# Adding up a tile's partial outputs in the second and third step of the following tile instead of the first and second

## The chip, the cores and the metric

The kernel runs on one core of one Trainium2 chip. The metric is the device time of one execution in microseconds (us), the median over several runs. The engines are called by the profile's names: PE (TensorE matmul) with PEld (its weight loads), DVE (VectorE), ACT (ScalarE), POOL (GpSimd) and SP (SyncE, which here only issues DMAs). A "q" behind an engine's name, as in SPq, is its sequencer.

## What is computed

Two branches over the same input of 2048 rows of 512 numbers, mixed by a gate per row. Branch A is an attention that goes through the rows in 64 segments of 32 and carries an 8-row memory from one segment to the next, so its segments can only be computed one after the other. Branch B is a layer norm with a two-layer MLP.

```python
for s in range(n_seg):                                   # 64 segments of 32 rows
    h = concat([mem, x[s*32:(s+1)*32]])                  # 8 memory rows + 32 rows
    q, k, v = h @ Wq, h @ Wk, h @ Wv                     # 32 heads of 128
    p = softmax(where(mask, q @ k.T * scale, -1e9))
    o = (p @ v) @ Wo                                     # 40 rows of 512
    mem = o[:8]                                          # carried on
    a[s] = o[8:]
b = gelu(layernorm(x) @ w1 + b1) @ w2 + b2
g = sigmoid((x * gate_w).sum(-1))
return g * a + (1 - g) * b
```

## The kernel before

**Tiles and steps.** 128 rows make a tile `T` (16 tiles), four segments make up a tile, and each segment `s = 4T + si` is one pass of the loop at line 694, called a step here; "the first step of a tile" is `si = 0`. Branch B runs ahead of the loop for all rows and leaves `(1 - g) * b` in DRAM (`c_dr`). The loop then takes some 10 us a step, and its order is written out by hand: each engine does its instructions in the order in which the code issues them, and waits on semaphores where an operand is not ready. The order within DVE's own instructions is therefore fixed by the code, and so is the order of the DMAs on SP.

**A step on PE.** Queries and keys of the step (line 124, into the PSUM banks `U`, from the transposed input `hT` of the step), scores (294, 298), values (143), sums of the exponentials (305, 308, 645), the product with the values (318, 323), then `wo_pass` (lines 674 to 680, matmuls at 155 into the bank `W`) and three little products (`new_mem`, line 688), from which DVE copies the new memory rows into the next step's `hT` (line 690). The first query matmul of the next step needs these copies. Between these parts PE runs work of the neighbouring tile that nothing in the step waits for (the generator `fill`: `left_qk`, `left_v`, `wo_left`).

**A delayed normalisation.** The softmax sums of the 32 ordinary rows are not divided out within the step. DVE takes the reciprocal (656), SP writes it to DRAM (659, `r_dr`) and reads it back spread over all partitions (660, `Rb`, 512 KB), and in the following step POOL multiplies (`x_norm`, line 672) the raw product `XR` by it into `UT` and `UL`. `wo_pass` of the following step reads that `UT`. After this POOL adds to `racc` (664) and copies parts of the next queries and inputs (278 `prep_q`, 274 `prep_h`).

**Outputs by parts.** What `wo_pass` leaves (`w`, 128 x 512) holds a step's output rows as four partial sums, one per group of heads. SP writes it to DRAM (`put_w`, line 243, in the step after the next) and reads it back so that the four parts of a row lie side by side in the tile `G` (`get_w`, 252; in each step of tile T + 1, the buffers of `G` are two). Eight rows of each segment come by another way: `wo_left` computes them a tile later, `put_left` (246) writes them to `l_dr` in the last step of tile T + 1, and `get_left` (254 to 257) reads them into `G` by four DMAs in the first step of tile T + 2. In that step SP also issues a DMA transpose of an input tile (`load_xT`, 98) while tiles are left to load.

**The addition.** `add_parts` (259 to 270) is a generator with four pieces: three additions of 128 x 512 (261, 263, 265) and a last one (268) that multiplies by the gate, adds `c`, and has SP store the tile (269). Lines 785 and 786 take two pieces in each step until none is left, right after `x_raw`; on DVE they stand behind `mask_put(0)` (287, called at 663) and ahead of the copies of line 690. The tiles 0 to 13 are finished in this way, 14 times; the last two tiles otherwise.

```python
        if si == 0 and T >= 2:
            get_left(T - 2)
            adds = add_parts(T - 2)
...
        x_raw(s)
        for _ in range(2):
            next(adds, None)
```

Of the kernel before, what the change touches and what calls it, by code (L numbers as in the profile page):

```python
# [27 lines left out]
def kernel(ctx, tc, A_x, A_mem0, A_Wq, A_Wk, A_Wv, A_Wo, A_seg_len, B_x, B_w1, B_b1, B_w2, B_b2, gate_w, out):  # L28
# [67 lines left out]
    def load_xT(T):  # L96
        xT = ew.tile([P, KC, P], BF16, tag="xT", bufs=3, name="xT")
        nc.sync.dma_start_transpose(out=xT[:], in_=x2[T * P:(T + 1) * P, :])
        xTs[T] = xT
# [21 lines left out]
    def qk_unit(bk, G, t, hf, kc):  # L121
        h0, h1 = HF[hf]
        for j in range(4):
            nc.tensor.matmul(bk[32 * j:32 * j + 32, :], lhsT=G[:, kc, :], rhs=W5[t][:, kc, h0:h1, j, :],  # L124
                             start=(kc == 0), stop=(kc == KC - 1), tile_position=(0, 32 * j))
# [37 lines left out]
    def flush(q, n=1):  # L163
        for _ in range(min(n, len(q))):
            q.pop(0)()
# [17 lines left out]
    def vp_load(T, si):  # L183
        nc.sync.dma_start(VP[T % 2][:, si].rearrange("p v e -> p (v e)"), VLs[T][si:P:SPT].rearrange("p a v e -> p a (v e)"))
# [20 lines left out]
    def c_load(T):  # L205
        c = cw.tile([P, Dm], BF16, tag="c", name="c")
        nc.sync.dma_start(c[:], c_dr[T * P:(T + 1) * P, :])
        cs[T] = c
# [32 lines left out]
    def put_w(s, w):  # L241
        T, si = divmod(s, SPT)
        nc.sync.dma_start(w_dr[T % 2][si], w[:])

    def put_left(T):
        nc.sync.dma_start(l_dr[T % 2][:], wls.pop(T)[:])

    def get_w(s):
        T, si = divmod(s, SPT)
        if si == 0:  # L250
            Gs[T] = cw.tile([P, 4, Dm], BF16, tag="G", name="G")
        nc.sync.dma_start(Gs[T][seg * si:seg * si + RIDE], w_dr[T % 2][si].rearrange("(c r) e -> r c e", c=4)[M:32])

    def get_left(T):
        for si in range(SPT):
            nc.sync.dma_start(Gs[T][seg * si + RIDE:seg * si + seg],
                              l_dr[T % 2][:].rearrange("(c i m) e -> i m c e", c=4, i=SPT)[si])

    def add_parts(T):
        a, G = cw.tile([P, Dm], FP32, tag="acc", bufs=1, name="acc"), Gs.pop(T)  # L260
        nc.vector.tensor_tensor(out=a[:], in0=G[:, 0], in1=G[:, 1], op=ALU.add)
        yield
        nc.vector.tensor_tensor(out=a[:], in0=a[:], in1=G[:, 2], op=ALU.add)
        yield
        nc.vector.tensor_tensor(out=a[:], in0=a[:], in1=G[:, 3], op=ALU.add)
        yield
        o = cw.tile([P, Dm], BF16, tag="o", name="o")
        nc.vector.scalar_tensor_tensor(out=o[:], in0=a[:], scalar=g_all[:, T:T + 1], in1=cs.pop(T)[:], op0=ALU.mult, op1=ALU.add)
        nc.sync.dma_start(out2[T * P:(T + 1) * P, :], o[:])
        yield  # L270

    def prep_h(s):
        T, si = divmod(s, SPT)
        nc.gpsimd.tensor_copy(out=hT[s % 3][:, :, 0:RIDE], in_=xTs[T][:, :, seg * si:seg * si + RIDE])
# [10 lines left out]
    def mask_put(i2):  # L285
        c = 4 * EW + (NG + 2 * M if i2 == 0 else 0)
        nc.vector.tensor_copy(out=(SbF, W)[i2][:, 0:c], in_=MkF[:, 0:c])
# [337 lines left out]
    def side(T, si):  # L625
        gens = []
        if si == 2:
            if T >= 1:
                gens.append(wo_left(T - 1, X1))
        elif T + 1 < NT:  # L630
            gens = [[left_qk(T + 1, 0, 0, X1), left_qk(T + 1, 1, 0, X2)], [left_qk(T + 1, 0, 1, X1), left_qk(T + 1, 1, 1, X2)], [],
                    [left_v(T + 1, 0, X1), left_v(T + 1, 1, X2)]][si]
        return chain(*gens)
# [33 lines left out]
    def x_norm(s):  # L667
        T, si = divmod(s, SPT)
        XR, Rb = XRs.pop(s), Rbs.pop(s)[:].rearrange("p (c q) (h j) -> p h j c q", c=4, h=2)
        for out, o, a, b in ((UT[(s + 1) % 2], M, LEFT, 32), (UL[T % 2], LEFT * si, 0, LEFT)):  # L670
            for h in range(2):
                nc.gpsimd.tensor_tensor(out=out[:, :, 4 * h:4 * h + 4, o:o + b - a], in0=XR[:, :, 4 * h:4 * h + 4, a:b], in1=Rb[:, h, :, :, a:b], op=ALU.mult)  # L672
# [21 lines left out]
    for s in range(nseg):  # L694
        T, si = divmod(s, SPT)
        last = s == nseg - 1
        hc, hn = hT[s % 3], hT[(s + 1) % 3]
        fill = side(T, si)
        if s + 1 < nseg:
            prep_h(s + 1)  # L700
        if s >= 1:
            x_norm(s - 1)
        if si == 0 and T >= 2:
            c_load(T - 2)
        if si < 3:
            vp_load(T, si + 1)
        if last:
            c_load(T - 1)
            c_load(T)
        if si == 0 and T + 2 < NT:  # L710
            load_xT(T + 2)
        if s >= 2 and s - 2 < SPT * (NT - 2):
            put_w(s - 2, ws.pop(s - 2))
        if 4 <= s < SPT * (NT - 2) + 4:
            get_w(s - 4)
        if si == 3 and 1 <= T < NT - 1:
            put_left(T - 1)
        if si == 0 and T >= 2:
            get_left(T - 2)
            adds = add_parts(T - 2)  # L720
        for n, (t, hf) in enumerate(((0, 0), (1, 0), (0, 1), (1, 1))):
            bk = U[n]
            for kc in range(KC):
                qk_unit(bk, hc, t, hf, kc)
            if n == 0:
                flush(act_q, 9)
                flush(dve_q, 9)
            qk_tr(qk_cast(bk[:]), (QT, KT)[t], hf, LEFT * (1 - t))
            if n == 0:
                mask_put(1)  # L730
        V = cw.tile([P, NG, Dh], BF16, tag="V", name="V")
        E = cw.tile([P, NG, EW], BF16, tag="E", name="E")
        R = cw.tile([P, NG * 40], FP32, tag="R", name="R")
        Rs[s] = R
        xsum = SbF[:, 0:32 * NG].rearrange("p (i q) -> p i q", q=32)

        def exps(i2, x):
            c = slice(0, 40) if x else slice(40, EW)
            nc.scalar.activation(out=E[:, 4 * i2:4 * i2 + 4, c], in_=Sb[i2][:, :, c], func=ACTF.Exp, scale=scale)  # L739

        def msum(i2):
            sums(U[i2][:, 320:352].rearrange("p (i q) -> p i q", q=8), E[:, 4 * i2:4 * i2 + 4, :], 40, 48, 8, True)

        def mnorm(i2):
            r, e = RP[i2], E[:, 4 * i2:4 * i2 + 4, 40:56].rearrange("p i (a q) -> p i a q", q=8)
            nc.vector.reciprocal(out=r, in_=U[i2][:, 320:352])
            nc.vector.tensor_tensor(out=e, in0=e, in1=r.rearrange("p (i q) -> p i q", q=8).unsqueeze(2).to_broadcast([P, 4, 2, 8]), op=ALU.mult)

        scores(s, 0)
        nc.scalar.activation(out=E[:, 0:4, :], in_=Sb[0], func=ACTF.Exp, scale=scale)  # L750
        for kc in range(KC):
            v_unit(X1, hc, 0, kc)

        def v_cast(vb, h):
            i0 = 4 * vb + 2 * h
            nc.scalar.copy(out=V[:, i0:i0 + 2, :].rearrange("p i e -> p (i e)"), in_=(X1, X2)[vb][:, 256 * h:256 * h + 256])  # L756

        v_cast(0, 0)
        v_unit(X2, hc, 1, 0)
        if not last:  # L760
            xsums(E, 0)
            msum(0)
            mnorm(0)
        scores(s, 1)
        exps(1, 0)
        v_cast(0, 1)
        exps(1, 1)
        for kc in range(1, KC - 1):
            v_unit(X2, hc, 1, kc)
        if not last:  # L770
            msum(1)
            mnorm(1)
        v_unit(X2, hc, 1, KC - 1)
        for h in range(2):
            v_cast(1, h)
        if last:
            break
        run(2)
        xsums(E, 1)
        recip_x(s)  # L780
        av(s, V, E)
        for j in (0, 2, 1, 3):
            nc.scalar.copy(out=UT[s % 2][:, j, :, 0:M], in_=U[j][:, 0:NG * 40].rearrange("p (i q) -> p i q", q=40)[:, :, 32:40])  # L783
# [3 lines that stand above are left out]
        run(2)  # L787
        prep_q(s + 1)
        w = wo_pass(UT[s % 2], (0, P, 2 * P, Dm))
        if s >= 1:  # L790
            ws[s - 1] = w
        run(2)
        new_mem(w, hn, 0)
        run(1)
        new_mem(w, hn, 1)
        run(1)
        new_mem(w, hn, 2)
        for _ in fill:
            pass
        if si == 3 and T + 2 < NT:  # L800
            left_x(T + 2)
        flush(dve_q, 9)
        nc.vector.tensor_tensor(out=rmin[:, 0:RW], in0=rmin[:, 0:RW], in1=R[:, 0:RW], op=ALU.min)
        flush(act_q, 9)
# [174 lines left out]
```

## Time and profile before

| | |
|---|---|
| median of 3 runs | 780.61 us (780.25 to 785.62) |
| the profiled execution | 785.22 us |
| its span, first to last instruction | 782.9 us |
| mean granted TensorE clock | 0.991 |
| busy PE / PEld / DVE / ACT / POOL | 754.3 / 410.5 / 425.3 / 538.6 / 291.5 us |

The profiled execution's time is 2.3 us above its span. The four pieces of the addition come 14 times each; in the view that groups instructions by line (busy time and mean duration, then the idle time of the engine just before, and what ended it) they are:

```profile
L268 DVE SCALAR_TENSOR_TENSOR o<-acc,g_all,c 128x512 bf16<-128x512 f32 x14 | 11.2, 798 | 0.5
...
L265 DVE TENSOR_TENSOR acc<-acc,G 128x512 f32<-128x512 f32 x14 | 10.0, 712 | 0.0
L263 DVE TENSOR_TENSOR acc<-acc,G 128x512 f32<-128x512 f32 x14 | 9.8, 698 | 0.5
L261 DVE TENSOR_TENSOR acc<-G 128x512 f32<-128x512 bf16 x14 | 9.7, 692 | 29.9 <-DMA r_dr<-R 23.5 <-DMA G<-l_dr 6.4
```

In a row of a timeline the first two numbers are the start and the duration in us, both of a merged group where the count behind the x is over one; a bracket tells for how long the engine sat idle before it and what ended that.

### The profile page before, as it was taken

The page shows a single profiled execution, that of the slowest core. Times are in us where ns is not written, and L with a number is a line of the kernel's source. Part 1 is how long each engine was busy: PE and PEld are TensorE (multiplying, and loading weights), DVE is VectorE, ACT ScalarE, POOL GpSimd, SP SyncE. Part 2 cuts the span into 40 slices and gives each one's busy share as a digit, 9 for nine tenths or more (in the row PEclk, how much of TensorE's full clock was granted, in tenths as well). Part 3 has the DMA queues.
Part 4 walks back from the last instruction along what each step waited for, and adds up shares of the span by engine and source line. Part 5 has one row for each costly group of instructions (what it writes and reads, how often), then busy time and mean ns, then how long its engine had stood idle before and what let it go on. Part 6 is the DMA issues. An engine that isn't in the chain of part 4 may idle for free.

```text
span 782.9 us, 43891 instructions
## 1 busy us (share of the span) xinstructions
PE 754.3 (96%) x19074; PEld 410.5 (52%) x19074; DVE 425.3 (54%) x1470; ACT 538.6 (69%) x1631; POOL 291.5 (37%) x522
## 2 busy tenths in 40 slices
PE   7999999999999999999999899999999999999997
PEld 5666555554555555555545455555545555555443
DVE  5776354555555464646455455646464655555454
ACT  4666676776777777777767567777767776777663
POOL 4111034443434444434344333444333443434441
PEclk9999999999999999999999999999999999999999
DMA  6779421324332323334243332233332323332212
GB/s 194 274 242 399 129 80 48 98 91 112 99 111 86 82 95 112 98 96 114 73 94 93 110 94 82 90 112 94 97 112 75 97 89 111 98 105 86 81 41 59
DMA packets 71687, 87.10 MB, mean 111 GB/s; under 512 B 23545, under 2 KB 61410, under 8 KB 69954
## 3 DMA queue, kind: packets, MB, share of 16 engines
q1 hardware_dynamic: 69762, 81.36, 33.6%
q8 instruction: 151, 2.47, 1.4%
q0 software_dynamic: 784, 1.97, 0.8%
q10 hardware_dynamic: 944, 0.92, 0.4%
q14 instruction: 46, 0.38, 0.2%
HBM read 64.30 MB, written 13.63 MB: 100 GB/s over the span
## 4 chain that ended last, share of the span: by engine, by line
PE 88%; DMA 3%; ACT 2%; DVE 2%; SPq 2%; issue 2%; POOL 1%; DVEq 0%; ACTq 0%; POOLq 0%
PE U L124 28%; PE X L143 17%; PE W L155 14%; PE X L124 6%; PE U L503 5%; PE U L318 4%; PE X L155 3%; PE W L497 2%; PE SbF L497 2%; PE U L305 1%; PE W L294 1%; DMA r_dr<-R 1%; PE U L688 1%; ACT w L679 1%; PE SbF L294 1%
## 5 line engine op out<-in xcount | busy, mean ns | idle before, releaser
L672 POOL TENSOR_TENSOR UT<-XR,Rb 128x384 bf16<-128x384 bf16 x126 | 139.9, 1132 | 321.4 <-DMA Rb<-r_dr 279.3
L129 ACT CAST Tb<-U 128x512 bf16<-128x512 f32 x258 | 151.2, 586 | 94.1 <-PE U L124 93.7
L124 PEld LDWEIGHTS <-hT 128*32 128x32 bf16 x4096 | 104.5, 97 | 115.2 <-DVE hT L690 20.5
L124 PE MATMUL U<-Wq_sb,hT 128*32 128x512 bf16 x2048 | 137.2, 383 | 11.8 <-DVE hT L690 11.8
L143 PE MATMUL X<-Wv_sb,hT 128*32 128x512 bf16 x2048 | 144.2, 378 | 0.6 <-issue 0.6
L124 PE MATMUL U<-Wk_sb,hT 128*32 128x512 bf16 x2048 | 133.6, 381 | 0.0
L155 PE MATMUL W<-Wo_sb,UT 128*32 128x512 bf16 x2080 | 126.9, 384 | 1.7 <-POOL racc L664 1.2
L133 DVE STREAM_TRANSPOSE QT<-Tb 128x256 f32<-128x256 f32 x128 | 57.1, 446 | 85.2 <-ACT Tb L129 85.2
L756 ACT CAST V<-X 128x256 bf16<-128x256 f32 x256 | 88.7, 372 | 16.4 <-PE X L143 4.6
L155 PEld LDWEIGHTS <-UT 128*32 128x32 bf16 x2080 | 56.7, 97 | 60.8 <-issue 17.6
L690 DVE CAST hT<-U 128x8 bf16<-128x8 f32 x126 | 19.7, 164 | 116.1 <-PE U L688 111.2
L679 ACT CAST w<-W 128x128 bf16<-128x128 f32 (+1 forms) x192 | 46.0, 311 | 48.9 <-PE W L155 48.9
L651 ACT CAST XR<-U 128x256 bf16<-128x256 f32 x252 | 78.4, 434 | 0.0
L133 DVE STREAM_TRANSPOSE KT<-Tb 128x256 f32<-128x256 f32 x128 | 57.0, 445 | 28.9 <-ACT Tb L129 24.4
L672 POOL TENSOR_TENSOR UL<-XR,Rb 128x128 bf16<-128x128 bf16 x126 | 60.7, 506 | 0.0
L143 PEld LDWEIGHTS <-hT 128*32 128x32 bf16 x2048 | 46.1, 94 | 23.1 <-issue 2.2
L503 PE MATMUL U<-w_sb,hTm 128*128 128x512 bf16 (+1 forms) x176 | 52.5, 382 | 0.0
L664 POOL TENSOR_TENSOR racc<-racc,R 128x72 f32<-128x72 f32 x63 | 22.6, 359 | 76.6 <-PE U L323 62.7
L783 ACT CAST UT<-U 128x64 bf16<-128x64 f32 x252 | 35.3, 226 | 22.9 <-PE U L323 22.9
L497 PEld LDWEIGHTS <-w_sb 128*128 128x128 bf16 (+1 forms) x352 | 34.4, 102 | 19.9 <-issue 1.3
L739 ACT ACTIVATE E<-W 128x64 bf16<-128x64 f32 (+1 forms) x128 | 35.0, 273 | 12.2 <-PE W L298 12.1
L688 PEld LDWEIGHTS <-w 128*32 128x32 bf16 x1008 | 22.8, 93 | 37.1 <-ACT w L679 29.1
(160 smaller groups left out, 1231.8 us busy)
## 6 DMA issues: line engine op xcount, KB each, us to landing
Rb<-r_dr SPq DMA_DIRECT2D x63, 512.0 KB
w_dr<-w SPq DMA_DIRECT2D x56, 128.0 KB
G<-w_dr SPq DMA_DIRECT2D x56, 96.0 KB
Wv_sb<-in_A_Wv_dram SPq DMA_DIRECT2D x4, 1024.0 KB
Wq_sb<-in_A_Wq_dram SPq DMA_DIRECT2D x4, 1024.0 KB
Wk_sb<-in_A_Wk_dram SPq DMA_DIRECT2D x4, 1024.0 KB
Wo_sb<-in_A_Wo_dram SPq DMA_DIRECT2D x4, 1024.0 KB
VP<-VL SPq DMA_DIRECT2D x64, 64.0 KB
```

The costliest lines, as they stand in the source:

```text
L124: nc.tensor.matmul(bk[32 * j:32 * j + 32, :], lhsT=G[:, kc, :], rhs=W5[t][:, kc, h0:h1, j, :], start=(kc == 0), stop=(kc == KC - 1), tile_ ...
L129: nc.scalar.copy(out=Tb[:], in_=bk.rearrange("p (a b e) -> p a e b", a=8, b=2))
L133: nc.vector.transpose(out=dst[:, 8 * hf:8 * hf + 8, c0:c0 + 32, :].rearrange("p a r b -> p a (r b)").bitcast(FP32), in_=Tb[:].rearrange("p ...
L143: nc.tensor.matmul(bk[32 * j:32 * j + 32, :], lhsT=G[:, kc, :], rhs=Wv5[:, kc, 4 * vb:4 * vb + 4, j, :], start=(kc == 0), stop=(kc == KC - ...
L155: nc.tensor.matmul(bk[32 * c:32 * c + 32, :], lhsT=U_[:, j, i, :], rhs=Wo_sb[:, 4 * i + j, :], start=(n == 0), stop=(n == NW - 1), tile_po ...
L497: nc.tensor.matmul(hp[:rows, 0:TB * P], lhsT=w1_sb[:, kc, fc * P:fc * P + rows], rhs=yTs[blk][:, kc, :], start=(kc == 0), stop=(kc == KC - 1))
L503: nc.tensor.matmul(bp(blk, tt)[:], lhsT=hTm[blk % 2][:rows, fc, tt * P:(tt + 1) * P], rhs=w2_sb[:rows, fc, :], start=(fc == 0), stop=(fc = ...
L651: nc.scalar.copy(out=XR[:, j], in_=U[j][:, 0:NG * 40].rearrange("p (i q) -> p i q", q=40)[:, :, 0:32])
L672: nc.gpsimd.tensor_tensor(out=out[:, :, 4 * h:4 * h + 4, o:o + b - a], in0=XR[:, :, 4 * h:4 * h + 4, a:b], in1=Rb[:, h, :, :, a:b], op=ALU ...
L679: nc.scalar.copy(out=w[:, a:b], in_=W[:, a:b])
L756: nc.scalar.copy(out=V[:, i0:i0 + 2, :].rearrange("p i e -> p (i e)"), in_=(X1, X2)[vb][:, 256 * h:256 * h + 256])
L783: nc.scalar.copy(out=UT[s % 2][:, j, :, 0:M], in_=U[j][:, 0:NG * 40].rearrange("p (i q) -> p i q", q=40)[:, :, 32:40])
```

## The change

The generator is made in the second step of a tile instead of the first. The loop at lines 785 and 786 still takes two pieces in a step, so lines 261 and 263 run in the second step instead of the first, and lines 265, 268 and the store of 269 in the third instead of the second. `get_left` stays where it is.

```diff
         if si == 0 and T >= 2:
             get_left(T - 2)
+        if si == 1 and T >= 2:
             adds = add_parts(T - 2)
```

The order on each engine shows that nothing else moves. On DVE the two pairs stand at the same place of their step as before, one step later. On SP the store of line 269 now comes behind five DMAs that it used to precede: the loads and stores of lines 184, 243 and 252, and the pair 659 and 660 of the third step. PE, ACT and POOL have the order they had. The number of instructions on each engine is unchanged.

## The prediction

> **What bounds the kernel.** I began with the page: the engines' busy shares, then the chain of waits followed back from the end.
>
> ```profile
> span 782.9 us, 43891 instructions
> ...
> PE 754.3 (96%) x19074; PEld 410.5 (52%) x19074; DVE 425.3 (54%) x1470; ACT 538.6 (69%) x1631; POOL 291.5 (37%) x522
> ...
> PE 88%; DMA 3%; ACT 2%; DVE 2%; SPq 2%; issue 2%; POOL 1%; DVEq 0%; ACTq 0%; POOLq 0%
> ```
>
> PE sets the time. DVE is busy 54% of it, and 40 us of additions on it cost nothing as such: they count only where PE stands still for them. So the next view is that of waits (who waited for what, total us, times, longest).
>
> ```profile
> DVE acc L261 <- DMA r_dr<-R: 23.5, 10, 3.5
> ...
> PE U L124 <- DVE hT L690: 11.8, 12, 2.1
> ...
> DVE acc L261 <- DMA G<-l_dr: 6.4, 3, 2.7
> ```
>
> Twelve times PE idles in front of the first query matmuls, for DVE's copies of the new memory: 11.8 us in all. Thirteen times DVE idles in front of the first addition, 29.9 us in all. That line reads nothing but `G`, so whichever DMA the view names, what it waits for is the landing of `get_left`. Whether the two belong together is seen in the timeline of tile 2, first on DVE and SP, then on PE; the rows from 196 us on are the second step, those from 207 us on the third.
>
> ```profile
> 185.55 0.42 DVE L287 CAST SbF<-MkF 128x248 f32<-128x248 bf16 x1
> 188.47 0.69 DVE L261 TENSOR_TENSOR acc<-G 128x512 f32<-128x512 bf16 x1 [2.50 <-DMA G<-l_dr]
> 189.20 0.69 DVE L263 TENSOR_TENSOR acc<-acc,G 128x512 f32<-128x512 f32 x1
> 189.81 0.23 DVE L690 CAST hT<-U 128x8 bf16<-128x8 f32 x2
> ...
> 197.31 0.68 DVE L265 TENSOR_TENSOR acc<-acc,G 128x512 f32<-128x512 f32 x1
> 198.03 0.80 DVE L268 SCALAR_TENSOR_TENSOR o<-acc,g_all,c 128x512 bf16<-128x512 f32 x1
> 199.95 0.43 DVE L690 CAST hT<-U 128x8 bf16<-128x8 f32 x2 [1.13 <-PE U L688]
> ...
> 207.19 0.42 DVE L287 CAST SbF<-MkF 128x248 f32<-128x248 bf16 x1
> 210.46 0.44 DVE L690 CAST hT<-U 128x8 bf16<-128x8 f32 x2 [2.85 <-PE U L688]
> ```
>
> ```profile
> 184.21 1.36 SPq L256 DMA_DIRECT2D G<-l_dr  x4
> ...
> 198.27 0.32 SPq L660 DMA_DIRECT2D Rb<-r_dr  x1
> 198.85 0.34 SPq L269 DMA_DIRECT2D out_dram<-o  x1
> ```
>
> ```profile
> 188.78 0.20 PE L688 MATMUL SbF<-SelM,w 128*32 128x8 bf16 x8
> 190.02 1.05 PE L124 MATMUL U<-Wq_sb,hT 128*32 128x512 bf16 x16 [1.03 <-DVE hT L690]
> ...
> 200.13 0.20 PE L688 MATMUL SbF<-SelM,w 128*32 128x8 bf16 x8
> 200.18 1.11 PE L124 MATMUL U<-Wq_sb,hT 128*32 128x512 bf16 x16
> ```
>
> In the first step SP has the four reads of `get_left` out by 185.57; DVE, free since 185.97, stands until 188.47, does both additions until 189.89, and only then gets to line 690, whose last operand PE had finished at 188.98. PE idles 1.03 us. In the second step the other two pieces start the moment DVE is free, end at 198.83, and DVE then waits 1.13 us for PE, not PE for DVE. So the additions themselves fit into the gap; the wait ahead of them does not. Tile 14 has no further input tile to transpose in front of `get_left`, and there the first addition starts early enough:
>
> ```profile
> 698.50 0.69 DVE L261 TENSOR_TENSOR acc<-G 128x512 f32<-128x512 bf16 x1 [1.26 <-DMA G<-l_dr]
> ...
> 700.00 0.20 PE L688 MATMUL SbF<-SelM,w 128*32 128x8 bf16 x8
> 700.05 1.11 PE L124 MATMUL U<-Wq_sb,hT 128*32 128x512 bf16 x16
> ```
>
> PE goes on at once. The wait for `G` is thus what costs, in the tiles 2 to 13: twelve, the count of the wait row.
>
> **The change, part by part.** The wait removed: by the second step `G` has been complete for about 9 us (188.47 against some 197.3), so line 261 finds it there. What PE gains per tile is a little over the idle row, because the row counts from the modelled end of line 688. In the second step the query matmuls start 0.05 us after that group starts, in the first 1.24 us after it: 1.19 us, 0.16 more than the 1.03 shown. Against that, PE then meets the last copy of line 690 within its first sixteen matmuls (1.11 us instead of 1.05). So 11.8 + 12 x (0.16 - 0.06) = 13.0 us.
>
> The pair 261 and 263 in the second step: 0.69 + 0.73 = 1.42 us from start to end, where 265 and 268 took 1.52 and left DVE 1.13 us of waiting. Cost nothing; without that spare it would be 0.3 us a tile at most (1.42 less 1.13).
>
> The pair 265 and 268 in the third step: DVE is free there from 207.61 until 210.46, 2.85 us, and the pair takes 1.52. Spare 1.33 us; cost nothing, and at most 0.2 us x 14 if the cover were gone (1.52 less 1.33).
>
> POOL beside the additions is the part that speaks against the change:
>
> ```profile
> 197.37 0.90 POOL L278 COPY QT<-QL 128x128 f32<-128x128 f32 x1
> 198.22 0.73 POOL L274 COPY hT<-xT 128x96 bf16<-128x96 bf16 x1
> 202.68 2.21 POOL L672 TENSOR_TENSOR UT<-XR,Rb 128x384 bf16<-128x384 bf16 x2 [3.73 <-DMA Rb<-r_dr]
> ...
> 207.59 0.41 POOL L278 COPY QT<-QL 128x128 f32<-128x128 f32 x1
> 207.94 0.26 POOL L274 COPY hT<-xT 128x96 bf16<-128x96 bf16 x1
> ```
>
> Beside the additions the two copies take 0.90 and 0.73 us, in the third step without them 0.41 and 0.26. In the first step the additions came too late (188.47) to meet them, so this slowing is added once per tile, 0.96 us. It ends 3.73 us before POOL's next work can start, which waits for `Rb`: cost nothing, and 14 x 0.96 = 13.4 us if there were no such cover, which would eat the whole gain. The Trainium skill, "SBUF — State Buffer", section "Who interferes with whom", says that a DVE instruction with two SBUF inputs and a GpSimd instruction that reads SBUF exclude each other and that the second to come is blocked until the first ends. The rows above agree. By that rule taken as a price on the path the sum would lose the 13.4 us; by the idle row it loses none, and I go by the row.
>
> The store of line 269 leaves SP in the third step behind that step's `Rb`, as in the second step now (198.27, 198.85). The five DMAs that it lets pass were never late for it: it held SP 0.34 us. Nothing reads the output. Cost nothing, taken up as a rival below.
>
> What is late next: the normalisation. In the first step the reciprocals go to DRAM and back while `get_left` is in flight, and `wo_pass` of the second step needs the `UT` made from them. The stall of PE gave that transfer some 1.1 us which it now loses. For tile 2, tile 5 and tile 12 (the last row is `wo_pass` of tile 2's third step, used further below):
>
> ```profile
> 193.07 2.22 POOL L672 TENSOR_TENSOR UT<-XR,Rb 128x384 bf16<-128x384 bf16 x2 [6.21 <-DMA Rb<-r_dr]
> 197.36 1.91 PE L155 MATMUL W<-Wo_sb,UT 128*32 128x512 bf16 x32
> ...
> 321.85 2.21 POOL L672 TENSOR_TENSOR UT<-XR,Rb 128x384 bf16<-128x384 bf16 x2 [8.21 <-DMA Rb<-r_dr]
> 324.21 1.05 PE L155 MATMUL W<-Wo_sb,UT 128*32 128x512 bf16 x16
> ...
> 620.62 2.22 POOL L672 TENSOR_TENSOR UT<-XR,Rb 128x384 bf16<-128x384 bf16 x2 [7.61 <-DMA Rb<-r_dr]
> 623.47 0.83 PE L155 MATMUL W<-Wo_sb,UT 128*32 128x512 bf16 x12
> ...
> 207.60 2.19 PE L155 MATMUL W<-Wo_sb,UT 128*32 128x512 bf16 x32
> ```
>
> `UT` is ready 2.07, 0.15 and 0.63 us ahead of use. Taking 1.08 us (13.0 / 12) off, tile 2 keeps 1.0, tile 5 is 0.93 late, tile 12 0.45. These two are the shortest of the twelve that I found, the others resemble tile 2, so I give back 1.4 us. The bounds are 0 and 12 x 0.93 = 11.2 us, if all became like tile 5.
>
> The sum is 13.0 - 1.4 = 11.6 us. On the profiled execution that is 785.22 - 11.6 = 773.6. The median run is 4.6 us shorter than that execution; part of this may be the piece of slow clock that follows, which I therefore don't count: 780.61 - 11.6 = 769.0 us.
>
> **The rivals.** First, a further gain through the clock. The windows view (PE busy, PEld, DVE, ACT, POOL, granted clock, DMA) around the longest stall, tile 8:
>
> ```profile
> 441.90:445.30 3.40, 1.28 (x32) 0.76 (x32) 2.54 (x9) 0.93 (x2) 0.00 (x0) 1.00 0.38 146
> 445.30:448.70 3.40, 3.40 (x40) 1.37 (x32) 1.29 (x4) 1.17 (x2) 1.47 (x2) 0.50 0.33 102
> ```
>
> With PE busy only 1.28 of 3.40 us, the following 3.40 us run at half clock: 1.7 us lost. If the stall brought that on and the median run has it too, it goes along: 769.0 - 1.7 = 767.3, and with no give-back 765.9. The Trainium skill, "TensorE: Matmul & The Clock Gate", Part 1, lets the clock fall to half after at least one idle window of about 3.4 us. The longest stall is 2.1 us, so by that rule it did not bring it on and the forecast stays; the two windows suggest that it did. Chance 0.14.
>
> Second, the normalisation takes the stall's place in many tiles, since `get_left` slows the round trip of the reciprocals in the first step of every one. Up to 11.2 us come back, and the result lies between 769.0 and 778.8, around 774. For it: tiles 5 and 12. Against it: tile 2. Chance 0.17.
>
> Third, no gain: the landing of `get_left` was not what held PE, or the adjacent first copies of line 690 are late for another reason; 780.6. Against it speaks tile 14. That the change does not do what it says is excluded by the order on the engines. Chance 0.05.
>
> Fourth, slower: in the third step the 128 KB store now runs beside the return of `Rb`, POOL's `x_norm` of the fourth step slips, and `wo_pass` there waits. With the store behind it, the second step's `Rb` took from 198.27 to 202.68, 4.4 us. `UT` of that step was ready at 204.89, and `wo_pass` of the third step starts at 207.60: spare 2.7 us, and so much I take for the fourth. The gain is gone when each of 14 tiles waits 13.0 / 14 = 0.93 us, so from a delay of 3.6 us on. At 4.0 us it is 14 x 1.3 = 18.2 less 13.0, or 785.8 us. The second step bears the same store with spare left. Chance 0.03.
>
> **How the numbers follow.** The forecast with its own range (767.6 to 771.5, a give-back of 0 to about 4) has 0.61, the rivals 0.14, 0.17, 0.05 and 0.03. The range from 765 to 774 takes in the clock and half of the second rival, leaving out less than 2 in 10. A measurement of this kernel can tell about 1% (7.8 us) from no change, so the line lies at 772.8. Faster by more: 0.61 + 0.14 + 0.07 of the second rival = 0.82; within 1%: 0.10 + 0.05 = 0.15; slower: 0.03.
>
> **What would show it.** Right: PE's wait for line 690 falls from 12 times and 11.8 us to next to nothing; DVE's idle time ahead of line 261 falls from 29.9 us to about 0; POOL's copies of 278 and 274 take 0.90 and 0.73 us in the third step too. The give-back shows as PE waits at line 155 for POOL in second steps, the clock rival as the missing window at 0.50 near 445 us. I am wrong if PE still idles at line 124 in first steps, or if line 155 waits in most tiles.

## The result, and the profile after

| | before | after |
|---|---|---|
| median of 4 runs | 780.85 us (780.25 to 785.62) | 771.34 us (768.97 to 773.18) |
| the profiled execution | 785.22 us | 773.18 us |
| its span | 782.9 us | 771.4 us |
| mean granted TensorE clock | 0.991 | 0.996 |

The medians differ by 9.5 us, where 11.6 us had been predicted. The ratio over all the runs, not only the medians, is 0.9863, with a 95% interval of 0.9816 to 0.9911: the change makes the kernel faster by about 1%. The page of the profile after:

```profile
span 771.4 us, 43914 instructions
...
PE 751.8 (97%) x19074; PEld 409.3 (53%) x19074; DVE 428.2 (56%) x1470; ACT 538.7 (70%) x1631; POOL 303.4 (39%) x522
...
PE 94%; DMA 2%; issue 1%; DVE 1%; ACT 1%; POOL 1%; DVEq 0%; POOLq 0%; SPq 0%; ACTq 0%
```

PE's share of the chain rises from 88% to 94%, and DVE's and SP's shrink. The page counts 23 instructions more than before. They are semaphore instructions (13 more on SP, 11 more on ACT, one fewer on DVE); the counted work of the engines is the same. POOL is busy 11.9 us more with it: its copies now run beside the additions in two steps of a tile. The four pieces of the addition, by line:

```profile
L263 DVE TENSOR_TENSOR acc<-acc,G 128x512 f32<-128x512 f32 x14 | 11.2, 799 | 0.5
L268 DVE SCALAR_TENSOR_TENSOR o<-acc,g_all,c 128x512 bf16<-128x512 f32 x14 | 11.1, 794 | 0.5
...
L261 DVE TENSOR_TENSOR acc<-G 128x512 f32<-128x512 bf16 x14 | 9.9, 708 | 0.0
L265 DVE TENSOR_TENSOR acc<-acc,G 128x512 f32<-128x512 f32 x14 | 9.7, 696 | 0.0
```

They cost DVE about what they did (41.9 us, 40.7 before), but the 29.9 us for which it stood ahead of line 261 are 0.0. What PE waits for, in the view of waits:

```profile
PE W L294 <- issue: 2.2, 4, 0.7
...
PE U L124 <- DVE hT L690: 0.4, 2, 0.2
PE W L155 <- POOL racc L664: 0.4, 1, 0.4
```

The row that carried the prediction (11.8 us, 12 times) is down to 0.4 us, twice. At the top of PE's rows now stands a wait of another kind, put down to "issue": PE waits for nothing that the profile shows. Other lines have it too. The last row is in tile 15, and before has it there too. Tile 2 on DVE shows the additions in their new places, in the second step (from 197 us) and the third (from 207 us):

```profile
188.79 0.43 DVE L690 CAST hT<-U 128x8 bf16<-128x8 f32 x2 [2.62 <-PE U L688]
...
197.25 0.68 DVE L261 TENSOR_TENSOR acc<-G 128x512 f32<-128x512 bf16 x1
197.97 0.80 DVE L263 TENSOR_TENSOR acc<-acc,G 128x512 f32<-128x512 f32 x1
199.91 0.43 DVE L690 CAST hT<-U 128x8 bf16<-128x8 f32 x2 [1.14 <-PE U L688]
...
207.48 0.68 DVE L265 TENSOR_TENSOR acc<-acc,G 128x512 f32<-128x512 f32 x1
208.20 0.80 DVE L268 SCALAR_TENSOR_TENSOR o<-acc,g_all,c 128x512 bf16<-128x512 f32 x1
210.41 0.43 DVE L690 CAST hT<-U 128x8 bf16<-128x8 f32 x2 [1.41 <-PE U L688]
```

All three copies of line 690 now wait for PE. On PE the second step of tile 2 begins at 189.03, 0.05 us after line 688, and then loses 0.75 us in its middle:

```profile
188.98 0.20 PE L688 MATMUL SbF<-SelM,w 128*32 128x8 bf16 x8
189.03 1.11 PE L124 MATMUL U<-Wq_sb,hT 128*32 128x512 bf16 x16
...
193.90 0.27 PE L294 MATMUL W<-QT,KT 128*32 128x40 bf16 x13
194.92 0.20 PE L294 MATMUL W<-QT,KT 128*32 128x40 bf16 x3 [0.75 <-issue]
```

How often that happens is seen from the windows view, taken step by step: tile 3, first to fourth step, each from its first query matmul to that of the next (stretch and length, then busy time of PE, PEld, DVE, ACT and POOL, granted clock, DMA share, GB/s). Before:

```profile
220.93:232.02 11.09, 10.38 (x300) 5.46 (x293) 6.01 (x21) 8.50 (x26) 4.06 (x7) 1.00 0.42 130
232.02:242.18 10.16, 10.16 (x288) 5.49 (x292) 6.70 (x22) 6.84 (x23) 5.01 (x7) 1.00 0.29 90
242.18:253.12 10.94, 10.74 (x300) 5.53 (x298) 5.59 (x20) 7.53 (x24) 3.96 (x7) 1.00 0.35 117
253.12:263.35 10.23, 10.23 (x300) 5.42 (x296) 4.65 (x17) 7.43 (x24) 4.36 (x8) 1.00 0.15 47
```

After:

```profile
220.88:231.11 10.23, 10.23 (x300) 5.41 (x296) 4.65 (x17) 7.67 (x25) 4.02 (x7) 1.00 0.50 129
231.11:241.94 10.83, 10.37 (x301) 5.48 (x297) 6.98 (x22) 7.68 (x25) 4.97 (x7) 1.00 0.35 95
241.94:252.85 10.91, 10.71 (x300) 5.51 (x296) 7.18 (x22) 7.52 (x24) 4.95 (x7) 1.00 0.34 104
252.85:263.08 10.23, 10.23 (x301) 5.43 (x296) 4.65 (x17) 7.43 (x24) 4.34 (x8) 1.00 0.20 63
```

An undisturbed step takes 10.23 us. The first step falls from 11.09 to that, the second rises from 10.16 to 10.83, and the third and fourth stay. The same was done for all steps of the tiles 2 to 13, with the time above 10.23 us summed over the twelve tiles, for every kernel that is told of below. The last column adds up PE's waits for "issue" within these tiles, from 0.07 us up; the view of waits leaves out those under 0.15 us.

| us above 10.23 a step, 12 tiles | first | second | third | fourth | sum | PE "issue": us, times |
|---|---|---|---|---|---|---|
| before | 14.3 | 1.5 | 4.6 | 0.0 | 20.4 | 2.47, 8 |
| after | 0.9 | 4.5 | 4.5 | 0.0 | 9.9 | 5.05, 16 |
| x0_after_again | 1.0 | 4.6 | 3.3 | 0.6 | 9.5 | 4.69, 12 |
| x1_transpose_behind | 3.8 | 1.3 | 3.5 | 0.3 | 9.0 | 2.77, 7 |
| x4_left_earlier | 0.8 | 1.7 | 6.1 | 0.7 | 9.3 | 3.45, 13 |
| x8_one_more_addition | 0.9 | 2.9 | 4.5 | 0.2 | 8.4 | 3.03, 13 |
| x9_three_more | 1.2 | 15.0 | 0.6 | 0.8 | 17.5 | 3.38, 11 |
| x3_third_fourth | 2.8 | 5.4 | 5.5 | 0.0 | 13.7 | 7.41, 19 |
| x5_extra_burst | 1.0 | 6.1 | 3.3 | 0.0 | 10.5 | 5.95, 13 |
| x2_transpose_third | 0.8 | 1.9 | 2.3 | 0.0 | 5.1 | 1.96, 7 |
| x6_left_earlier_late_adds | 0.7 | 3.0 | 4.9 | 0.8 | 9.5 | 4.17, 10 |
| x7_both_moved | 1.0 | 1.0 | 1.7 | 0.5 | 4.2 | 1.75, 5 |
| x10_parts_before_rb | 5.4 | 1.8 | 2.3 | 0.3 | 9.9 | 2.32, 7 |
| x11_all_moved | 1.5 | 0.6 | 2.9 | 0.0 | 5.1 | 1.83, 7 |

The two runs of the changed kernel (after and x0) show how far a figure scatters by itself: by 1.2 us in the third steps, by 0.1 in the second. These are two profiles only.

The 1.5 of before holds 1.7 us of a stretch at half clock, the one shown in the prediction near 445 us; without it the second steps lost nothing (-0.2). Before had another such stretch behind the twelve tiles:

```profile
735.80:739.20 3.40, 2.29 (x92) 1.16 (x80) 2.19 (x9) 2.05 (x11) 2.51 (x5) 0.95 0.06 9
739.20:742.60 3.40, 3.26 (x32) 1.08 (x24) 1.04 (x2) 1.12 (x5) 1.21 (x2) 0.55 0.50 165
```

After has neither. The step that began at 444.28 in before, with the longest stall ahead of it, begins at 439.98 in after:

```profile
436.40:439.80 3.40, 3.40 (x98) 1.76 (x83) 0.80 (x5) 2.41 (x13) 0.91 (x3) 1.00 0.19 52
439.80:443.20 3.40, 3.40 (x80) 1.70 (x72) 2.71 (x10) 2.47 (x6) 0.00 (x0) 1.00 0.53 165
```

So the span of the profiled executions goes from 782.9 to 771.4 like this: 13.4 us less in first steps (14.3 to 0.9), 3.4 less for two stretches at half clock of 1.7 each, 4.7 more in second steps (-0.2 to 4.5), and 0.6 more in small pieces, nearly all ahead of and behind the twelve tiles.

### The profile page after: what moved, and what is told of

Read it like the earlier page. It is cut to its first block, busy times and chain, and to the rows that moved or that the text cites. A ratio compares the mean times of both kernels' runs of the same rounds, so it can differ in the third digit from the quotient of the medians.

```text
span 771.4 us, 43914 instructions
## 1 busy us (share of the span) xinstructions
PE 751.8 (97%) x19074; PEld 409.3 (53%) x19074; DVE 428.2 (56%) x1470; ACT 538.7 (70%) x1631; POOL 303.4 (39%) x522
## 3 DMA queue, kind: packets, MB, share of 16 engines
q8 instruction: 151, 2.47, 1.4%
## 4 chain that ended last, share of the span: by engine, by line
PE 94%; DMA 2%; issue 1%; DVE 1%; ACT 1%; POOL 1%; DVEq 0%; POOLq 0%; SPq 0%; ACTq 0%
PE U L124 29%; PE X L143 18%; PE W L155 15%; PE X L124 7%; PE U L503 5%; PE U L318 4%; PE X L155 4%; PE SbF L497 2%; PE W L497 2%; PE U L305 1%; PE W L294 1%; PE U L688 1%; PE SbF L294 1%; PE SbF L645 1%; DMA b1r<-in_B_b_dram 1%
## 5 line engine op out<-in xcount | busy, mean ns | idle before, releaser
L740 ACT ACTIVATE E<-W 128x64 bf16<-128x64 f32 (+1 forms) x128 | 35.0, 273 | 15.7 <-PE W L298 14.8
```

## The experiments

Two questions were open. Was it the wait for `get_left`, and not the place of the additions, that cost 13 us? And why do the second steps lose 4.7 us? Ratios are to the kernel before, run beside them on the same chip: x0, x1, x3 and x4 on one (its median there 778.02 us), x2, x5, x6 and x7 on another (779.85), x8 to x11 on a third (779.94).

### The wait or the work

**x0_after_again**: the changed kernel, unedited, beside the three that follow.

> The changed kernel once more, beside the next three on one chip. 771 us (769 to 773), 9 to 10 us below the kernel before. Its second steps of the tiles 2 to 13 should again be longer than 10.23 us on average (10.6), with PE waiting for its own instruction stream ('issue') inside them.

Measured: 771.62 us, ratio 0.9902 (0.987 to 0.9935). That is the time expected, but only 6.4 us below the kernel before and not 9 to 10: here before has 778.02 us, 2.8 us less than in the first comparison. The gain by medians is thus 6.4 to 9.5 us.

**x1_transpose_behind**: the kernel before with its additions in the first and second step; in the first step the DMA transpose of line 98 is issued behind `get_left` instead of ahead of it.

```diff
-        if si == 0 and T + 2 < NT:
-            load_xT(T + 2)
...
         if si == 0 and T >= 2:
             get_left(T - 2)
             adds = add_parts(T - 2)
+        if si == 0 and T + 2 < NT:
+            load_xT(T + 2)
```

> The kernel before, additions in the first and second step as there; only the DMA transpose of the first step is issued behind get_left instead of ahead of it. Theory 'the wait costs, not the additions': get_left goes out 2.1 us earlier, the first addition starts by about 8 us into the step instead of 9.7, PE's wait for line 690 falls from 11.8 us to under 2, and the time is that of the changed kernel, 771 (769 to 773). Rival 'the additions themselves are too much for the first step': PE goes on waiting, 779 to 781.

Measured: 772.16 us, ratio 0.9925 (0.9897 to 0.9954). The view of waits:

```profile
DVE acc L261 <- DMA G<-l_dr: 13.7, 10, 2.0
...
PE U L124 <- DVE hT L690: 2.2, 7, 0.6
...
DVE acc L261 <- DMA r_dr<-R: 1.6, 1, 1.6
```

DVE still waits, but half as long (15.3 us against 29.9 before), and PE meets only 2.2 us of it (under 2 was expected). First steps fall from 14.3 to 3.8.

**x4_left_earlier**: the kernel before, additions unmoved; `get_left` is issued one step earlier, in the last step of the tile before, behind `put_left`.

```diff
             put_left(T - 1)
+            get_left(T - 1)
...
         if si == 0 and T >= 2:
-            get_left(T - 2)
             adds = add_parts(T - 2)
```

> The kernel before, additions in the first and second step as there; get_left is issued in the last step of the tile ahead, right behind put_left, so G is complete long before the first addition. Theory 'the wait costs': no wait of PE for line 690, 13 us less. Theory 'code load' adds: with get_left out of the first step the reciprocals' round trip starts 1 us or more earlier and the second steps lose part of their 0.37 us: 767 to 770. Rival 'the additions themselves': 779 to 781.

Measured: 771.17 us, ratio 0.9893 (0.9856 to 0.993). The view of waits:

```profile
PE U L124 <- DVE hT L690: 0.4, 2, 0.2
...
DVE acc L261 <- DMA G<-w_dr: 0.2, 1, 0.2
```

With the data there in time, the pair in the first step costs PE nothing. The time is above the 767 to 770 us that were expected: the second steps do lose less (1.7 us against 4.5 in after), but the third lose more (6.1 against 4.5). x1 and x4 take off what the change takes off, without moving one addition, and their intervals overlap with that of x0: it was the wait.

**x8_one_more_addition** and **x9_three_more**: after, with the addition of line 261 done twice, and four times, into the same output. They measure the 1.13 us that the prediction counted as DVE's spare in the second step.

```diff
         nc.vector.tensor_tensor(out=a[:], in0=G[:, 0], in1=G[:, 1], op=ALU.add)
+        nc.vector.tensor_tensor(out=a[:], in0=G[:, 0], in1=G[:, 1], op=ALU.add)
```

(x9 has three such lines more instead of one.)

> The changed kernel with line 261 done twice in each tile (the same sum again, 0.7 us more of DVE in the second step). Theory 'the additions fit, the wait did not': DVE's spare there is 1.13 us, so nothing changes: 771 (769.5 to 773), PE's wait for line 690 under 1 us.

> The changed kernel with line 261 done four times (2.1 us more of DVE in the second step). Theory 'the additions fit, the wait did not': the spare of 1.13 us is overrun by 0.95 us in each of 14 tiles; PE's wait for line 690 comes back with 11 to 13 us, and the time goes to 780 to 785, somewhat less where such a stall covers code loads. Rival 'additions are free anywhere': 771.

Measured: x8 770.62 us, ratio 0.9867 (0.9824 to 0.9911); x9 780.87 us, ratio 0.9994 (0.9966 to 1.0023). In the timeline of x8's tile 2 the copies of line 690 still wait for PE, 0.42 us:

```profile
196.33 0.68 DVE L261 TENSOR_TENSOR acc<-G 128x512 f32<-128x512 bf16 x1
197.04 0.80 DVE L262 TENSOR_TENSOR acc<-G 128x512 f32<-128x512 bf16 x1
197.88 0.69 DVE L264 TENSOR_TENSOR acc<-acc,G 128x512 f32<-128x512 f32 x1
198.99 0.44 DVE L691 CAST hT<-U 128x8 bf16<-128x8 f32 x2 [0.42 <-PE U L689]
```

In x9 the spare is used up, and the wait row of before is back, in the second step and for work alone:

```profile
PE U L124 <- DVE hT L693: 11.1, 14, 1.2
```

An addition of some 0.7 us is thus free where 1.1 us are spare. Three of them, 2.1 us, overrun the spare by about 1 us a tile, and that is paid. x9's step table shows something else: its second steps are 10.5 us longer than after's (15.0 against 4.5), but its third steps 3.9 us shorter (0.6 against 4.5). A stall ahead of a step takes the losses out of that step, as it did in the second steps of before.

### What the second steps lose

PE's waits for "issue" are waits for its own instructions. PE has 19074 matmuls and as many weight loads; the page of after counts 151 packets and 2.47 MB on a queue of kind "instruction", which is 16 KB a packet and some 250 of PE's instructions. Two things in the traces tie the waits to these packets. Counted along PE's matmuls and weight loads, the waits stand whole packets apart: those at line 294 in the tiles 2 to 5 of after are 2300 instructions from one to the next, which is nine times 255.6, and in each of the fourteen kernels all the waits of the last column fall on one place of such a block, to within three instructions. And in the twelve kernels other than before and x9, each of the 103 waits of over 0.15 us in these tiles ends 1.2 to 1.6 us after the end of the last such packet.

Around the end of the first query and key matmuls of tile 2's second step the DMA view, over 1.2 us in 40 slices, shows one such packet, in before:

```profile
GB/s 171 103 580 69 68 34 34 68 34 0 34 34 0 0 0 0 0 0 0 0 0 0 0 0 0 0 0 0 0 0 0 0 0 0 0 17 0 17 0 17
...
q8 instruction: 1, 0.02, 5.2%
```

and in after:

```profile
GB/s 103 102 137 34 683 102 34 34 0 0 0 0 0 0 0 0 0 0 0 0 0 0 0 0 0 0 0 0 0 0 0 0 0 0 0 0 0 17 0 17
...
q8 instruction: 1, 0.02, 5.2%
```

Both views begin at 192.30 us, so the slice with the 16 KB starts at 192.36 before and 192.42 after, and 5.2% of sixteen engines over 1.2 us is one packet of 1.0 us. The packet comes at the same time, but PE began the step at 190.02 before and at 189.03 after. In before it arrived at 193.4 with PE still among the long matmuls, and line 294 ran without a gap; in after PE ran dry at 194.17 and went on at 194.92, 1.5 us after the packet's end. In each of the tiles 2 to 5 the second step of after has such a gap at line 294, of 0.75, 0.47, 0.48 and 0.52 us, which before has not, and in each the packet starts where the burst of transfers that begins with `Rb` ends. The Trainium skill, "Runtime: NRT & Kernel Launch", section "Instruction fetch mechanics", says that an engine's instructions are refilled in 16 KiB blocks of 256 by a DMA queue of its own while the current block runs, and that this is mostly hidden. The packets agree; hidden it is not quite, with 16 waits and 5.05 us in these twelve tiles of after.

Not all that the second steps lose shows as idle time: in after the waits in them come to 2.9 us of 4.5. But in the six tiles that have such waits (2 to 5, 10 and 11) the matmuls behind a wait come later in their step by more than the idle time shown, in tile 3 by 0.64 us for 0.47, and these six steps lose 4.1 us in all. Most of the rest is 0.36 us at the end of tile 9's second step, where PE waits for DVE's copies.

Three rivals for what makes the second steps lose: the additions beside POOL's copies in the second step; the bytes of the burst, behind which the packet would stand; the time at which `Rb` is issued.

**x3_third_fourth**: after, with the additions one step later still, in the third and fourth steps (the last tile keeps its place).

```diff
-        if si == 1 and T >= 2:
+        if si == (2 if T < NT - 1 else 1) and T >= 2:
             adds = add_parts(T - 2)
```

> The changed kernel with the additions one step later still, in the third and fourth step (for the last such tile in the second and third, because the loop ends before). Theory 'code load': the second steps' extra time (10.6 us instead of 10.23) comes from PE's instruction fetch, which stands behind the DMA burst of the first step, so it stays without the additions there: 771 (769.5 to 772.5), second steps about 10.6 us. Rival 'the additions beside POOL's copies make the second steps longer': these go back to 10.23 us, 12 x 0.37 = 4.5 us less: 767.

Measured: 773.3 us, a little above the 769.5 to 772.5 that was expected, ratio 0.9918 (0.9884 to 0.9953). Without any addition in them, the second steps lose 5.4 us. Contention between DVE and POOL there is not the cause.

**x5_extra_burst**: after, with a copy of 512 KB from DRAM to DRAM put right behind `Rb` in the first steps of the tiles 2 to 13 (`x_dr` is a DRAM tile that nothing reads).

```diff
+        if s % SPT == 0 and 2 <= s // SPT < NT - 2:
+            nc.sync.dma_start(x_dr[:], c_dr[0:4 * P, :].rearrange("(p a) d -> p (a d)", a=4))
```

> The changed kernel with one more DMA: in the first step of the tiles 2 to 13 SP copies 512 KB from DRAM to DRAM (128 rows of 4 KB, read by nobody) right behind the read of Rb. Theory 'code load behind the burst': the first instruction fetch inside the second step, now about 2.5 us (up to 3.4) after its start, moves to 4 us or later, PE runs dry in nearly every second step, their mean goes from 10.6 to 11.4 us or more, and the time from 771 to 780 or more, with PE's waits listed as 'issue'. Rival 'the fetch is as late as PE asks for it': second steps stay at 10.6 us, 771 to 773. If PE waits at line 155 for POOL instead, the burst held up Rb and the run says nothing on code.

Measured: 773.66 us, ratio 0.9917 (0.9883 to 0.9952). A miss: it was to be 780 us at least. The second steps go from 4.5 to 6.1 us and their gaps in tiles 2 to 5 from 2.2 to 3.5 us in all, the right way, but in tile 3 the packet moved only from 3.36 to 3.75 us into the step. The copy went out in packets of 32 KB, and `VP`, `w` and `G` stood behind it while the instruction packet did not. That the packet simply stands behind all bytes issued earlier is therefore wrong. PE waits for POOL nowhere at `wo_pass` in these tiles, so the copy did not hold up `Rb` for it.

**x2_transpose_third**, **x6_left_earlier_late_adds** and **x7_both_moved**: after, with the DMA transpose in the third step; with `get_left` a step earlier as in x4; with both. Each has `Rb` issued earlier in the first step: 9.80 us into it on average in after, 8.77, 9.11 and 8.83 in these three.

```diff
-        if si == 0 and T + 2 < NT:
+        if si == 2 and T + 2 < NT:
             load_xT(T + 2)
```

> The changed kernel with the DMA transpose of the first step moved to the third step. Theory 'code load behind the burst': Rb of the first step is issued about 1 us earlier (8.7 us into the step instead of 9.8), so the second steps' extra time falls from 4.5 us in twelve tiles to under 1.5; the third and fourth steps may take some of it over: 768 to 770. Rival: the second steps keep their 4.5 us, 771 to 772.

> The changed kernel (additions in the second and third step) with get_left issued a step earlier, right behind put_left. Theory 'code load behind the burst': as in the run with get_left earlier and the additions where they were, the second steps' extra time falls to about 1.7 us in twelve tiles; since the additions cost nothing at either place, the time is the same as that run's, 771 (769 to 772). Rival 'the place of the additions matters once the wait is gone': more than 3 us apart from it.

> The changed kernel with get_left a step earlier and the DMA transpose in the third step, so that the first step has neither. Theory 'code load behind the burst': Rb of the first step is issued about 8.3 us into it, the second steps come to 10.3 us, and the time to 766 to 769 unless the fourth steps, which now hold put_left and get_left, take it over. Rival: 771.

Measured: 767.78 us, ratio 0.9864 (0.9817 to 0.9911); 769.11 us, 0.9862 (0.9812 to 0.9912); 766.93 us, 0.9847 (0.9798 to 0.9896). The times are as expected (x2 just under its 768), but the second steps of x2 and x6 lose 1.9 and 3.0 us, more than the 1.5 and 1.7 that were forecast for them.

**x10_parts_before_rb** and **x11_all_moved**: after, and x7, with the DMAs of `put_w` and `get_w` moved on SP from behind `Rb` to between the write of `r_dr` and the read of `Rb`, where SP waits for the write anyway.

```diff
         # in recip_x, between the DMA of line 659 and that of line 660
+        if s >= 2 and s - 2 < SPT * (NT - 2):
+            put_w(s - 2, ws.pop(s - 2))
+        if 4 <= s < SPT * (NT - 2) + 4:
+            get_w(s - 4)
...
         # in the loop
-        if s >= 2 and s - 2 < SPT * (NT - 2):
-            put_w(s - 2, ws.pop(s - 2))
-        if 4 <= s < SPT * (NT - 2) + 4:
-            get_w(s - 4)
```

> The changed kernel with the store and load of the partial outputs (lines 243 and 252) issued between the store of the reciprocals and the read of Rb, in the 1.4 us in which SP waits for that store to land, in every step; so the burst that begins with Rb is shorter by 224 KB. Theory 'code load behind the burst': the first instruction fetch of a step comes about 1 us earlier, the extra time of second and third steps (4.5 and 4.5 us in twelve tiles) falls to 4 us in all or less: 765 to 768. Rival 'the fetch is as late as PE asks for it': 771. Rb itself may land up to 0.5 us later; if PE then waits at line 155 for POOL, the gain is smaller.

> The same, with get_left a step earlier and the DMA transpose in the third step as in the run with both moved (767). Theory 'code load behind the burst': what is left there, 4.2 us of extra time in the loop, falls further, to 763 to 766. Rival: 767.

Measured: 767.06 us, ratio 0.9812 (0.9766 to 0.9858); 766.25 us, ratio 0.9806 (0.9765 to 0.9847), a little above the 763 to 766 that was expected.

In all five the second steps lose less than in after (0.6 to 3.0 us against 4.5), and the waits for "issue" are fewer us too (1.8 to 4.2 against 5.05). What counts is seen when the 144 second steps of the twelve kernels other than before and x9 are put in order of the time at which the first instruction packet starts in them:

| packet starts, us into the second step | steps | us lost, mean | least to most |
|---|---|---|---|
| up to 2.2 | 49 | 0.05 | -0.07 to 0.36 |
| 2.2 to 2.7 | 36 | 0.13 | -0.07 to 0.76 |
| 2.7 to 3.1 | 27 | 0.41 | 0.02 to 0.81 |
| 3.1 to 4 | 23 | 0.73 | 0.52 to 1.16 |
| 4 and later | 9 | -0.03 | -0.07 to 0.01 |

In the nine steps of the last row another packet had started less than 0.9 us ahead of the step. So a second step loses when its packet comes late in it. That it comes late because of when `Rb` and what follows it go out, the third rival, fits all five runs (in x10 and x11 `Rb` is issued 9.17 and 8.95 us into the first step, on average), but is not shown: each of these edits moves several transfers at once. x11 is the fastest version that was run, by its median. Its interval lies clear of that of the changed kernel in x0 (0.987 to 0.9935) but not of that in the first comparison (0.9816 to 0.9911), and x2, x7, x10 and x11 can't be ranked against each other.

x10's first steps lost 5.4 us, and there the view of waits has `PE U L305 <- ACT E L740`, in two waits of 2.1 us, the longer of 1.5 us in tile 7. The windows around it:

```profile
390.00:393.40 3.40, 2.06 (x80) 1.28 (x83) 1.34 (x6) 1.91 (x10) 2.62 (x6) 0.95 0.20 45
393.40:396.80 3.40, 3.40 (x40) 1.36 (x36) 0.00 (x0) 1.10 (x4) 0.39 (x2) 0.55 0.56 177
```

This is the third case in which a stretch of PE busy well under its 3.40 us (1.28, 2.29, 2.06) is followed by one at half clock. x5's profiled execution has a fourth: 2.34 us busy of the 3.40 from 725.30 us on, then 3.40 us at a clock of 0.50.

But a low share of PE alone does not make it: in before PE is busy for 2.31 of the 3.41 us from 397.52 us on, and in x9 for 2.17 of those from 451.94 us on, and the clock of the next 3.41 us is 1.00 in both.

## Why the prediction came out right, point by point

**The wait removed: right, in cause and size.** 13.0 us were predicted, 11.8 from the row of waits and 1.2 carried over from the rows of tile 2 to all twelve; the first steps gave 13.4. The cause is shown twice: x4 takes the wait away and x1 half of it, and both leave the additions; x9 leaves the data early and brings the wait back with work.

**The pair in the second step, the pair in the third: right, nothing.** The spare was put at 1.13 and 1.33 us; after shows 1.14 and 1.41 us left over in tile 2, and x8 put 0.7 us more into the first without a cost. The prediction's ceilings for the loss of this cover (0.3 and 0.2 us a tile) are not sound: they take away spare time that was counted behind a pair already running there. Without any spare a pair would cost its whole 1.4 or 1.5 us. Nothing hung on them.

**POOL beside the additions: right, hidden.** In the third step of after the copies take what the second step's took, and POOL's next work still starts 3.35 us after they end. The timeline of tile 2:

```profile
207.55 0.90 POOL L278 COPY QT<-QL 128x128 f32<-128x128 f32 x1
208.40 0.73 POOL L274 COPY hT<-xT 128x96 bf16<-128x96 bf16 x1
212.48 2.23 POOL L672 TENSOR_TENSOR UT<-XR,Rb 128x384 bf16<-128x384 bf16 x2 [3.35 <-ACT Tb L129]
```

0.41 and 0.26 us became 0.90 and 0.73, and POOL's busy time rose by 11.9 us (13.4 was the estimate); none of it is on the path. The prediction reads its rows as agreeing with a rule by which the second to come stands until the first has ended. They agree that the two slow each other, but not in size: the copies were longer by 0.49 and 0.47 us, where 0.62 and 0.61 us of an addition were still to run when they started. POOL's times are rough in these traces.

**The store of line 269: right, nothing.** Fourth steps stay at 10.23 us, so the rival in which it delays `Rb` has nothing for it.

**What is late next: this step failed.** The prediction gave back 1.4 us because `UT` would come too late in tiles like 5 and 12, as if `Rb` came at a fixed time on the clock. In after no matmul of line 155 waits for `UT` in the second steps of the tiles 2 to 13. In tile 5 POOL and PE have

```profile
319.17 2.19 POOL L672 TENSOR_TENSOR UT<-XR,Rb 128x384 bf16<-128x384 bf16 x2 [6.34 <-DMA Rb<-r_dr]
```

```profile
323.11 1.91 PE L155 MATMUL W<-Wo_sb,UT 128*32 128x512 bf16 x32
```

with `UT` ready 1.75 us ahead of use, where before had left 0.15 and the prediction -0.93. `Rb`, issued at 314.48 instead of 315.44, came 4.7 us after its issue instead of 6.4. In tile 12 it was 3.8 instead of 6.1. Its round trip was not fixed, and the two long ones of before did not return at their places. With that the second rival, the same mechanism in most tiles, falls too. What did come back was 4.7 us instead of 1.4, some 4.1 of it through waits that the profile of before could not show in their place, since the stall covered them: PE's waits for instructions in second steps. There the question "what else was the stall hiding?" was asked of `UT` alone.

**The clock, taken as a rival with 0.14: it came true in the profiled execution.** Both stretches at half clock are gone there (the rival had named the one near 445 us), 3.4 us that the forecast didn't count. That is why its 773.6 us for the profiled execution lies so near the measured 773.18, and it is luck: two misses, 3.3 us of give-back too little (4.7 against 1.4) and 3.4 of clock not counted, cancel. Without the clock the parts give 13.4 - 4.7 - 0.6 = 8.1 us, and the medians fell by 9.5 us and, beside x0, by 6.4, against a forecast of 11.6; the time came out 2.3 us above the 769.0 predicted, inside the range. The Trainium skill, "TensorE: Matmul & The Clock Gate", Part 1, asks for an idle window of some 3.4 us before the clock halves; here stalls of at most 2.1 us stood ahead of the two stretches in question (near 445 us and in x10), so the traces speak for less than that. That the stall of before brought on the stretch near 445 us is likely from four such pairs of windows, not shown: no experiment made it come and go, and the two windows of before and x9 named above were as little busy as the fourth pair's and stayed at full clock.

**Still open** is why the instruction packet of the second step starts when it does. Settled are that the step loses the more the later it starts, from 2.2 us on, that it starts at about the same time with and without the stall (in the tiles 2 to 6 within 0.5 us, counted from the start of the first step), that a stall ahead of a step covers it (before, x9), that the additions have no part in it (x3), and that 512 KB more in the burst moves it only by tenths of a microsecond (x5). Which engine or ring carries it can't be seen in these traces.

## What to carry to other kernels

When an in-order engine shows a wait, look at what is queued behind the waiting instruction: 12 us here came from small copies behind an addition that stood for its data, not from 40 us of additions. Three cures did the same (the work later, its DMA earlier, another DMA out of its way), so try the DMA before the work. And before a removed stall is counted as gain, ask of everything that went on during it, the engine's own instruction fetch included, whether it is now late.

## What was not expected of the hardware

- PE's instructions come in packets of 16 KB that take about 1.0 us, and PE went on 1.2 to 1.6 us after the end of one that it had waited for. It ran dry for 0.07 to 0.75 us at a time, 16 times in twelve tiles of after, four of them in a stretch of many small matmuls at line 294.
- The read of `Rb` (512 KB) took 4.7 us from issue to use in one kernel and 6.4 in the other, at the same place of tile 5.
- A stretch of some 3.4 us at half clock followed windows in which PE had been busy for 38% (1.28 of 3.40 us), 61%, 67% and 69% of the time; after two others, at 64% (x9) and 68% (before), the clock stayed full.
